# Between attention and experts: counts summed by matmul, steps in another order, slot numbers converted one scatter sooner

## The chip, the cores and the metric

One Trainium2 chip, one core. The metric is device time in microseconds (us) of one execution, the median over runs. The engines are named as in the profile: PE (TensorE), DVE (VectorE), ACT (ScalarE), POOL (GpSimd), SP (the queue that issues most transfers).

## The reference

Three stages follow each other; the output of one is the input of the next.

```
attn = hash_bucket_attention(q, k, v, proj)       # 2 x 8 heads, 768 positions, head size 64
x    = attn as 1536 tokens x 512

logits = x @ w_gate                               # 1536 x 8
e_idx  = argmax(logits)                           # one expert for each token
out[t] = gate_w[t] * sigmoid(x[t] @ w_output_gate)[e_idx] * (relu(x[t] @ w1[e]) @ w2[e])

h = out @ w_in;  solu = h * softmax(h);  y = layernorm(solu) * g_ln @ w_out
```

## The kernel before

The 1536 tokens are 12 tiles of 128. Attention works through 96 units (a head and a block of 128 queries each); three tiles of tokens become ready together, tiles 6 to 8 and then 9 to 11 last. Everything is issued in an order written out by hand, and each engine runs its instructions in that order. The change lies wholly in the stretch between the last attention unit and the first expert, some 10 us long.

In that stretch each token needs its expert and its row ("slot") among the tokens of this expert. The steps, by name:

- `route_a(i)` on DVE: the maximum of the logits and a one-hot row for each token (`oh_all`). The argument is a part: part 2 is tiles 6 to 8, part 3 is tiles 9 and 10, part 4 is tile 11.
- `route_mm(i)` on PE: small matmuls that add up, for each expert, the tokens that come before this one: a triangular matrix times the one-hots, `ones` times `hs` (the counts of earlier parts) and `ones` times single one-hot tiles (the list `before`, L787).
- `route_b(i)` on DVE: picks the own expert's sum from PSUM, which is the slot number (`slot_f`, L803). Then, on POOL and tile by tile, it converts the number to an integer (L809) and starts an indirect scatter (L811) of 128 token rows to `xs` in DRAM.
- `route_s(g)` on DVE: adds the counts of a group of three tiles to `hs` (L822, L823).

Expert 0 does not go through DRAM for tiles 6 to 11. Its input is gathered on PE: `gather_first` (4 matmuls with an identity, L945) brings in what earlier tiles gave, then `gm(t)` (8 matmuls a tile, L952) multiplies the tokens of tile t by a one-hot matrix that `oh(t)` has made (on DVE, L936, or on ACT, two operations at L933 and L934). `gather_copy` copies the four PSUM results out, blocks 0 and 3 on ACT (L963), blocks 1 and 2 on DVE (L961), into `xw`, which `mm1(0, ...)` reads as its moving operand, block 0 first. Expert 1 and later experts read `xs` back through a transposing DMA, `x_load` (L1126); that of expert 1 waits until all scatters have landed.

The PSUM tiles: the gather's blocks 0 and 3 are two banks of one tile of pool `ps_s` (two buffers of two banks, used in turn), blocks 1 and 2 are `ps_t`. The last attention result, `pv`, and `route_mm(4)` have a `ps_s` tile each. When the experts begin, the pool `ps_x` of eight banks takes the place of all of these, and its first tile lies on the first bank of `ps_s`; a tile of the new pool waits for all readers of the old tile that lies below it. The count of `ps_s` allocations (one in `first`, 96 for the units, then `pv`, gather, `route_mm(4)`) puts the gather's tile of this kernel on the first buffer.

After the gather the order is: the four `mm1` groups of expert 0, those of expert 1, `mm2` of expert 0, `mm1` of expert 2, and so on, then the last stage. `fin_*` are the steps that turn a finished attention result into tokens and logits: `fin_hi`/`fin_lo` split it into two halves, `fin_r` takes reciprocals, `fin_mm` multiplies by the gate weights, `fin_l` and `fin_x` scale logits and tokens.

Of the kernel before, what the change touches and what calls it, by code (L numbers as in the profile page):

```python
# [8 lines left out]
F32 = mybir.dt.float32  # L9
F16 = mybir.dt.float16  # L10
I32 = mybir.dt.int32
# [10 lines left out]
def kernel(  # L22
# [15 lines left out]
    nc = tc.nc  # L38
# [3 lines left out]
    E, _, FF = w1.shape  # L42
    NS = S // 128
    NTILE = NT // 128
# [6 lines left out]
    CAP = 224  # L51
# [15 lines left out]
    const = ctx.enter_context(tc.tile_pool(name="const", bufs=1))  # L67
# [5 lines left out]
    xs = dram.tile([E * NT, 2 * DM], F16, name="xs")  # L73
# [5 lines left out]
    ones16 = const.tile([128, 128], F16, name="ones16")  # L79
# [5 lines left out]
    hs = const.tile([128, 5, E], F16, name="hs")  # L85
    oh_all = const.tile([128, NTILE, E], F16, name="oh_all")
    slot_f = const.tile([128, NTILE], F32, name="slot_f")
    slot_all = const.tile([128, NTILE], I32, name="slot_all")
    me = const.tile([128, NTILE, 2], F32, name="me")
    pos_all = const.tile([128, NTILE], I32, name="pos_all")  # L90
    tok = const.tile([128, NTILE], I32, name="tok")
# [210 lines left out]
    scattered = []  # L302
# [9 lines left out]
    def attention(es):  # L312
# [326 lines left out]
        def emit_pv(x):  # L639

            n, blk, qt, _ = units[pairs[x][0]]
            j = 2 * n + blk
            last = x == NU // 2 - 1
            if last:
                pv[j, 2] = ps_s.tile([128, 2, 512], F32, tag="s", name="s")[:, 0]
            elif qt == 0:
                pv[j, 0] = ps_v.tile([128, SB], F32, tag="v", name="v")
            o = pv[j, 2][:, 0:128] if last else pv[j, 0][:, qt * 128:(qt + 1) * 128]
            vt = ldt[n, "v"]
            ph = [pt.pop(i) for i in pairs[x]]  # L650
            for c in range(NS):
                for h in range(2):
                    nc.tensor.matmul(o[64 * h:64 * h + 64], vt[:, h, c], ph[h][:, c],  # L653
                                     start=(c == 0), stop=(c == NS - 1), tile_position=(0, 64 * h))
# [117 lines left out]

        rmm = {}

        def route_mm(i, before=(), tail=False, own=False):

            t0, nt = parts[i]
            if own:
                m = ps_s.tile([128, 2, 512], F32, tag="s", name="s")[:, 0]
            elif tail:  # L780
                m = ps_v.tile([128, 512], F32, tag="v", name="v")
            else:
                m = ps_m.tile([128, 512], F32, tag="m", name="m")
            oh = oh_all[:, t0:t0 + nt]
            nc.tensor.matmul(m[:, 0:nt * E], upper, oh, start=True, stop=False)
            for t in before:
                nc.tensor.matmul(m[:, 0:nt * E], ones16, oh_all[:, t:t + 1].to_broadcast([128, nt, E]),  # L787
                                 start=False, stop=False)
            nc.tensor.matmul(m[:, 0:nt * E], ones16, hs[:, min(i, 3), None].to_broadcast([128, nt, E]),
                             start=False, stop=(nt == 1))  # L790
            for t in range(1, nt):
                nc.tensor.matmul(m[:, t * E:nt * E], ones16,
                                 oh[:, t - 1:t].to_broadcast([128, nt - t, E]), start=False, stop=(t == nt - 1))
            rmm[i] = m

        def route_b(i, before=()):
            t0, nt = parts[i]
            d = nc.vector
            m = rmm.pop(i)
            oh = oh_all[:, t0:t0 + nt]  # L800
            pr = t3("rpr", nt, E, bufs=1)
            for t in range(nt):
                d.scalar_tensor_tensor(out=pr[:, t], in0=m[:, t * E:(t + 1) * E], scalar=1.0, in1=oh[:, t],  # L803
                                       op0=ALU.mult, op1=ALU.mult, accum_out=slot_f[:, t0 + t:t0 + t + 1])
            for f in before:
                f()
            for t in range(nt):
                so = slot_all[:, t0 + t:t0 + t + 1]
                nc.gpsimd.tensor_scalar(out=so, in0=slot_f[:, t0 + t:t0 + t + 1], scalar1=1.0, scalar2=1.0,  # L809
                                        op0=ALU.mult, op1=ALU.mult)  # L810
                x = nc.gpsimd.indirect_dma_start(  # L811
                    out=xs[:, :], out_offset=bass.IndirectOffsetOnAxis(ap=so, axis=0),
                    in_=xh[divmod(t0 // 3, 2)][:, t0 % 3 + t].rearrange("p a b -> p (a b)"), in_offset=None).ins
                for y in scattered:
                    tc.declare_no_dep(x, y, reason="every token has a row of its own")
                scattered.append(x)

        def route_s(g):
            d = nc.vector
# [213 lines left out]
    with tc.manual_schedule():  # L1033
        with ExitStack() as es:
            A = attention(es)
            pj = A["pj"]
            cm, rb, rg = A["cm"], A["rb"], A["rg"]
            setup_first()
            A["first"]()
            A["load"](1)  # L1040
            A["at"](2, setup_late)
            NU = A["NU"]
            bg = A["bg"]
            JL = 2 * NP - 2
            a_ = A.__getitem__
            pv, fa, tr = a_("emit_pv"), a_("fin_a"), a_("emit_t")
            due = a_("due")
            J = JL + 1
            for i in range(NU):
                a_("emit_s")(i, a_("steps_t")(i - 2) if 2 <= i else iter(()))  # L1050
                due(i, 0)
                a_("emit_max")(i)
                due(i, 1)
                if i == NU - 1:
                    tr(NU - 2)
                a_("emit_exp")(i)
                if i == 5 or i >= 6 and i % 2 == 0:
                    pv(i // 2 - 2)
                due(i, 2)
            assert not bg, bg.keys()  # L1060

            oh, gm = a_("gather_oh"), a_("gather_mm")
            pv(NU // 2 - 2)
            a_("fin_l")(JL)
            a_("fin_x")(JL)
            a_("fin_r")(J, 0, 2)
            a_("fin_hi")(J, 0, 2, True)
            tr(NU - 1)
            a_("fin_lo")(J, 0, 2)
            a_("fin_mm")(J, 0, 2)  # L1070
            a_("route_a")(2)
            pv(NU // 2 - 1)
            a_("fin_hi")(J, 2, 3, True)
            a_("gather_ps")()
            a_("gather_first")(range(4))
            a_("route_mm")(2, tail=True)
            a_("fin_l")(J, 0, 2)
            a_("fin_x")(J, 0, 2, True)
            a_("fin_r")(J, 2, 3)
            a_("fin_lo")(J, 2, 3)  # L1080
            a_("route_b")(2)
            a_("fin_mm")(J, 2, 3)
            oh(6)
            oh(7, True)
            a_("route_s")(2)
            gm(6, range(4))
            a_("route_a")(3)
            oh(8, True)
            a_("route_mm")(3, tail=True)
            a_("fin_l")(J, 2, 3)  # L1090
            gm(7, range(4))
            a_("route_a")(4)
            gm(8, range(4))
            a_("route_mm")(4, (9, 10), tail=True, own=True)
            a_("route_b")(3)
            oh(9)
            oh(10, True)
            lo = a_("fin_x")(J, 2, 3, True, True)
            gm(9, range(4))
            a_("route_b")(4, before=(lambda: oh(11), lo))  # L1100
            gm(10, range(4))
            a_("route_s")(3)
            gm(11, (0, 3, 1, 2))
            a_("totals_mm")()
            a_("route_d")(0, 0, 1)
            a_("gather_copy")()
            a_("totals")()
            for x in range(2):
                a_("route_d")(x + 1, 0, 1)
            for x in range(3):  # L1110
                a_("route_d")(x, 2, 3, 4)
# [41 lines left out]
        def overflow():  # L1153
            why = "made on the chip from token counts"
            n = nc.values_load(win[:, 3:4], min_val=0, max_val=MW, skip_runtime_bounds_check_because=why)
            with tc.If(n != 0), tc.For_i(0, n, 1) as i:
# [48 lines left out]
                for a in range(2):  # L1205
                    nc.vector.tensor_copy(out=yT[:, a, :, bass.ds(c0, WIN)], in_=yt[:, a * KD:(a + 1) * KD])

        def mm1(e, g, n):
            w = wt["w1", e].rearrange("p a (k f) -> p a k f", k=KD)
            xw = xw_t[e][..., 0:n]  # L1210
            if g == 0:
                hh_t[e] = mp.tile([128, 2, KF, CAP], F16, tag="hh", name="hh")
            ps = ps_a.tile([128, 2, CAP], F32, tag="a", name="a")
            for i in range(2):
                fs = slice((2 * g + i) * 128, (2 * g + i + 1) * 128)
                for kk in range(KD):
                    nc.tensor.matmul(ps[:, i, 0:n], w[:, 0, kk, fs], xw[:, 0, kk], start=(kk == 0), stop=False)  # L1217
                    nc.tensor.matmul(ps[:, i, 0:n], w[:, 0, kk, fs], xw[:, 1, kk], start=False, stop=False)  # L1218
                    nc.tensor.matmul(ps[:, i, 0:n], w[:, 1, kk, fs], xw[:, 0, kk], start=False, stop=(kk == KD - 1))  # L1219
            return ps  # L1220
# [287 lines left out]
```

## Time and profile before

| | |
|---|---|
| median of 3 runs | 514.83 us (514.05 to 515.08) |
| the profiled execution, its own time | 513.23 us |
| its span, first to last instruction | 511.5 us |
| granted PE clock, mean | 0.999 |
| PE busy | 496.9 us, 97% of the span |
| DVE, ACT, POOL busy | 388.2, 320.9, 281.9 us |

PE is the engine that runs nearly all the time. Busy time of PE overlaps from one matmul to the next, so what counts in the rows below is the start of each matmul and the idle time in square brackets, with the instruction that ended it.

### The profile page before, as it was taken

Reading aid. Unit: us, or ns where it says so; the run is one execution under the profiler, and the core shown is the slowest. Engines: PE = TensorE matmul, PEld = TensorE weight load, DVE = VectorE, ACT = ScalarE, POOL = GpSimd, SP = SyncE. Lnnn points to the kernel's source line nnn. Section 1 sums busy time; section 2 is a strip of 40 time slices with the busy share of each in tenths; the row PEclk is TensorE's granted clock in tenths of the full one; section 3 lists DMA queues with packets and bytes.
Section 4 is the critical chain, followed back from the end, with each engine's and each line's share of the span. In section 5 each row is a group of like instructions: output and inputs, shape, how many; then the busy total and the mean of one; then the engine's idle time right before and its main releaser. Section 6 shows DMA issues by size and latency. Waiting matters only on the chain. (4 is left out here: it accounts for less than half of the span.)

```text
span 511.5 us, 12503 instructions
## 1 busy us (share of the span) xinstructions
PE 496.9 (97%) x4716; PEld 385.1 (75%) x4716; DVE 388.2 (76%) x922; ACT 320.9 (63%) x601; POOL 281.9 (55%) x438
## 2 busy tenths in 40 slices
PE   7899999999999999999999999999999999999994
PEld 5678787888888887887999999999984444444443
DVE  7787888888889888877779799979935987656610
ACT  6778787887887788886256566556623445534421
POOL 6999897869879898644366587322012113221131
PEclk9999999999999999999999999999999999999999
DMA  7398969772946675500499999998800246442281
GB/s 263 57 214 185 245 162 232 195 204 78 187 142 108 187 202 121 161 1 22 157 305 278 318 309 271 268 324 277 279 12 0 42 82 97 108 106 62 62 145 41
DMA packets 107182, 83.21 MB, mean 163 GB/s; under 512 B 80624, under 2 KB 89456, under 8 KB 107120
## 3 DMA queue, kind: packets, MB, share of 16 engines
q1 hardware_dynamic: 104816, 76.09, 59.1%
q0 software_dynamic: 2304, 6.31, 3.2%
q8 instruction: 37, 0.61, 0.5%
q14 instruction: 25, 0.20, 0.1%
HBM read 51.43 MB, written 9.97 MB: 120 GB/s over the span
## 5 line engine op out<-in xcount | busy, mean ns | idle before, releaser
L629 PE MATMUL t<-ident,p 128*128 128x128 f32 x576 | 126.1, 275 | 0.6
L617 ACT ACTIVATE p<-s,mx 128x768 f32<-128x768 f32 x96 | 95.8, 998 | 36.4 <-DVE mx L606 22.5
L602 DVE TENSOR_REDUCE mx<-s 128x1 f32<-128x768 f32 x96 | 91.5, 953 | 28.4 <-PE s L592 22.4
L631 ACT COPY pt<-t 128x384 f32<-128x384 f32 x192 | 85.6, 480 | 7.4 <-PE t L629 6.2
L629 PEld LDWEIGHTS t<-ident,p 128*128 128x128 f32 x576 | 77.8, 141 | 15.6 <-ACT pt L631 9.0
L653 PE MATMUL v<-pt,v 128*64 128x128 f32 x1128 | 72.0, 277 | 0.0
L653 PEld LDWEIGHTS v<-pt,v 128*64 128x64 f32 x1128 | 60.6, 137 | 7.7 <-issue 6.8
L1446 PE MATMUL o<-wo,zT 128*128 128x512 f16 (+1 forms) x312 | 63.7, 363 | 0.1
L1246 PE MATMUL a<-hh,wb 128*128 128x224 f16 (+5 forms) x256 | 63.4, 251 | 0.1
L131 POOL TENSOR_SCALAR dm<-dm 128x512 f32<-128x512 f32 x16 | 33.0, 2061 | 55.5 <-ACT dm L126 55.3
L1374 PE MATMUL h<-wi,yT 128*128 128x512 f16 x288 | 63.5, 379 | 0.0
L1247 PE MATMUL a<-hh,wb 128*128 128x224 f16 (+5 forms) x256 | 63.4, 251 | 0.0
L1248 PE MATMUL a<-hh,wb 128*128 128x224 f16 (+5 forms) x256 | 63.4, 251 | 0.0
L592 PE MATMUL s<-k,q 128*128 128x384 f16 x192 | 59.0, 329 | 1.2 <-ACT p L617 1.2
L592 PE MATMUL s<-b,cm 128*128 128x384 f16 x192 | 57.2, 326 | 0.9 <-DVE b L554 0.9
L1219 PE MATMUL a<-xw,wa 128*128 128x224 f16 (+5 forms) x224 | 55.1, 249 | 0.0
L1218 PE MATMUL a<-xw,wa 128*128 128x224 f16 (+5 forms) x224 | 55.1, 249 | 0.0
L1217 PE MATMUL a<-xw,wa 128*128 128x224 f16 (+5 forms) x224 | 55.1, 249 | 0.0
L1446 PEld LDWEIGHTS <-zT 128*128 128x128 f16 x312 | 30.5, 98 | 32.2 <-issue 0.4
L1374 PEld LDWEIGHTS <-yT 128*128 128x128 f16 x288 | 28.2, 98 | 33.7
L1452 POOL DMA_INDIRECT out_dram<-o,tok x12 | 12.6, 1048 | 53.3 <-issue 42.4
L168 ACT ACTIVATE wb<-raw 128x1024 f16<-128x1024 f32 x24 | 25.3, 1055 | 22.1 <-DMA raw<-in_moe_w_dram 22.0
(275 smaller groups left out, 1017.7 us busy)
## 6 DMA issues: line engine op xcount, KB each, us to landing
raw<-in_moe_w_dram SPq DMA_DIRECT2D x64, 512.0 KB, 6.1
raww<-in_moe_w_in_dram SPq DMA_DIRECT2D x8, 512.0 KB, 5.1
raww<-in_moe_w_out_dram SPq DMA_DIRECT2D x8, 512.0 KB, 6.4
xs<-raw SPq DMA_DIRECT2D x8, 448.0 KB, 4.4
v<-in_v_dram SPq DMA_DIRECT2D x8, 384.0 KB, 6.7
q<-in_q_dram SPq DMA_DIRECT2D x6, 384.0 KB, 4.3
k<-in_k_dram SPq DMA_DIRECT2D x6, 384.0 KB, 6.5
cm<-q SPq DMA_DIRECT2D x14, 96.0 KB, 2.1
```

Source lines behind the costliest of these rows:

```text
L592: nc.tensor.matmul(t[:, c, 0:SB], d[x, h][:, s], flat(d[y, h])[:, c * SB:(c + 1) * SB], start=first, stop=not first)
L602: nc.vector.tensor_reduce(out=mx[:, 0:1], in_=t[:, :, 0:SB], op=ALU.max, axis=AX.XY)
L617: nc.scalar.activation(out=p, in_=s_t.pop(i)[:, :, 0:SB], func=AF.Exp, scale=mx[:, 1:2], bias=mx[:, 2:3], accum_out=sums[j][:, qt, h:h + 1])
L629: nc.tensor.transpose(t[:, g * 128:(g + 1) * 128], p[:, c, g * 128:(g + 1) * 128], ident)
L631: nc.scalar.copy(out=pt[i][:, 3 * c:3 * c + 3], in_=t[:, 0:SB].rearrange("p (g c) -> p g c", g=3))
L653: nc.tensor.matmul(o[64 * h:64 * h + 64], vt[:, h, c], ph[h][:, c], start=(c == 0), stop=(c == NS - 1), tile_position=(0, 64 * h))
L1217: nc.tensor.matmul(ps[:, i, 0:n], w[:, 0, kk, fs], xw[:, 0, kk], start=(kk == 0), stop=False)
L1246: nc.tensor.matmul(ps, w[:, 0, f, ds], hh[:, 0, f], start=(f == 0), stop=False)
L1247: nc.tensor.matmul(ps, w[:, 0, f, ds], hh[:, 1, f], start=False, stop=False)
L1248: nc.tensor.matmul(ps, w[:, 1, f, ds], hh[:, 0, f], start=False, stop=(f == KF - 1))
L1374: nc.tensor.matmul(ps[:, c], yT[:, a, kk, ts], w_i[:, w, kk, c * 512:(c + 1) * 512], start=(kk == 0 and a == 0 and w == 0), stop=(kk == KD ...
L1446: nc.tensor.matmul(ps, zT[:, KF * a + f], w_o[:, w, f, cs], start=(f == 0 and a == 0 and w == 0), stop=(f == KF - 1 and a == 1))
```

## The change

In the stretch named above:

1. `route_mm(2)` is issued ahead of `gather_first`, not behind it. On DVE `route_b(2)` and `oh(6)` come ahead of `fin_r` and `fin_lo` of tile 11; `gm(6)` comes ahead of `fin_mm` of tile 11 on PE.
2. `route_s(2)` moves from between `oh(6)` and `route_a(3)` to the end, just ahead of `route_s(3)`. So `hs` lacks the counts of tiles 6 to 8 when `route_mm(3)` and `route_mm(4)` run, and they add them by matmuls: three more each.
3. The gather's PSUM tile is taken ahead of the last `pv` tile, so the two swap buffers; `route_mm(4)` uses the second bank of the `pv` tile instead of a tile of its own. The first three PSUM tiles of expert 0 are taken together and used in the order second, third, first.
4. For tiles 6 to 11 POOL converts the slot numbers of the next tile before it starts the scatter of a tile. Ahead of the last scatter it writes one element with a `memset`.

```
-                pv[j, 2] = ps_s.tile([128, 2, 512], F32, tag="s", name="s")[:, 0]
+                m = ps_s.tile([128, 2, 512], F32, tag="s", name="s")
+                pv[j, 2], pv[j, 2, 1] = m[:, 0], m[:, 1]
...
-        def route_mm(i, before=(), tail=False, own=False):
+        def route_mm(i, before=(), tail=False, own=None):
-            if own:
-                m = ps_s.tile([128, 2, 512], F32, tag="s", name="s")[:, 0]
+            if own is not None:
+                m = pv[own, 2, 1]
...
-            nc.tensor.matmul(m[:, 0:nt * E], ones16, hs[:, min(i, 3), None].to_broadcast([128, nt, E]),
+            nc.tensor.matmul(m[:, 0:nt * E], ones16, hs[:, min(i, 2), None].to_broadcast([128, nt, E]),
...
-            for t in range(nt):
-                so = slot_all[:, t0 + t:t0 + t + 1]
-                nc.gpsimd.tensor_scalar(out=so, in0=slot_f[:, t0 + t:t0 + t + 1], scalar1=1.0, scalar2=1.0,
+            for t in range(t0, t0 + nt):
+                nc.gpsimd.tensor_scalar(out=slot_all[:, t:t + 1], in0=slot_f[:, t:t + 1], scalar1=1.0, scalar2=1.0,
                                         op0=ALU.mult, op1=ALU.mult)
...
+                if i < 2:
+                    scatter(t)
+                else:
+                    if held:
+                        scatter(held.pop())
+                    held.append(t)
+            if t == NTILE - 1:
+                nc.gpsimd.memset(slot_all[0:1, NTILE:NTILE + 1], 0)
+                scatter(held.pop())
+
+        held = []
+
+        def scatter(t):
+            x = nc.gpsimd.indirect_dma_start(
+                out=xs[:, :], out_offset=bass.IndirectOffsetOnAxis(ap=slot_all[:, t:t + 1], axis=0),
+                in_=xh[divmod(t // 3, 2)][:, t % 3].rearrange("p a b -> p (a b)"), in_offset=None).ins
...
             a_("route_a")(2)
+            a_("gather_ps")()
             pv(NU // 2 - 1)
             a_("fin_hi")(J, 2, 3, True)
-            a_("gather_ps")()
+            a_("route_mm")(2, tail=True)
             a_("gather_first")(range(4))
-            a_("route_mm")(2, tail=True)
             a_("fin_l")(J, 0, 2)
             a_("fin_x")(J, 0, 2, True)
+            a_("route_b")(2)
+            oh(6)
+            oh(7, True)
+            gm(6, range(4))
             a_("fin_r")(J, 2, 3)
             a_("fin_lo")(J, 2, 3)
-            a_("route_b")(2)
             a_("fin_mm")(J, 2, 3)
-            oh(6)
-            oh(7, True)
-            a_("route_s")(2)
-            gm(6, range(4))
+            oh(8, True)
+            gm(7, range(4))
             a_("route_a")(3)
-            oh(8, True)
-            a_("route_mm")(3, tail=True)
+            a_("route_mm")(3, (6, 7, 8), tail=True)
             a_("fin_l")(J, 2, 3)
-            gm(7, range(4))
+            gm(8, range(4))
             a_("route_a")(4)
-            gm(8, range(4))
-            a_("route_mm")(4, (9, 10), tail=True, own=True)
+            a_("route_mm")(4, range(6, 11), tail=True, own=J)
             a_("route_b")(3)
             oh(9)
             oh(10, True)
...
             gm(10, range(4))
+            gm(11, (0, 3, 1, 2))
+            a_("route_s")(2)
             a_("route_s")(3)
-            gm(11, (0, 3, 1, 2))
             a_("totals_mm")()
...
+        ps0 = [ps_a.tile([128, 2, CAP], F32, tag="a", name="a") for _ in range(3)]
+        ps0 = ps0[1], ps0[2], ps0[0]
...
-            ps = ps_a.tile([128, 2, CAP], F32, tag="a", name="a")
+            ps = ps0[g] if e == 0 and g < 3 else ps_a.tile([128, 2, CAP], F32, tag="a", name="a")
```

## Rows read from the trace of the kernel before

**Rows 1.** Stretches: us, busy PE, PEld, DVE, ACT, POOL, PE clock, DMA share, GB/s.

```profile
250.00:255.00 5.00, 5.00 (x55) 5.00 (x53) 3.15 (x34) 1.19 (x8) 0.00 (x0) 1.00 0.48 102
330.00:367.00 37.00, 37.00 (x463) 36.93 (x461) 33.29 (x44) 24.69 (x36) 8.79 (x6) 1.00 0.92 287
367.00:500.00 133.00, 132.72 (x730) 67.22 (x728) 81.51 (x202) 54.42 (x81) 26.25 (x37) 1.00 0.37 79
```

**Rows 2.** Waits of PE from 236 to 256 us: total, times, longest.

```profile
PE a L1217 <- ACT raw L963: 0.7, 1, 0.7
PE s L952 <- DVE raw L936: 0.5, 1, 0.5
PE v L785 <- DVE oh_all L770: 0.3, 1, 0.3
```

**Rows 3.** Timeline of PE: start us, us, line, out<-in, count, [idle before <-releaser].

```profile
237.91 0.36 PE L945 MATMUL s<-raw,ident 128*128 128x448 f16 x1
...
238.67 0.18 PE L785 MATMUL v<-oh_all,upper 128*128 128x24 f16 x1
...
242.46 0.19 PE L787 MATMUL s<-oh_all,ones 128*128 128x8 f16 x2
...
242.62 0.35 PE L952 MATMUL s<-raw,xh 128*128 128x224 f16 x2
...
244.92 0.17 PE L859 MATMUL m<-hs,ones 128*128 128x8 f16 x1
245.75 0.26 PE L1217 MATMUL a<-raw,wa 128*128 128x224 f16 x1 [0.67 <-ACT raw L963]
...
264.15 0.26 PE L1246 MATMUL a<-hh,wb 128*128 128x224 f16 x1
```

**Rows 4.** Timeline of DVE, same columns.

```profile
238.03 0.16 DVE L689 TENSOR_SCALAR r<-sums 128x2 f32<-128x2 f32 x1
...
238.36 0.29 DVE L679 SCALAR_TENSOR_TENSOR xt<-s,xt 128x128 f16<-128x128 f32 x1
238.97 0.17 DVE L803 SCALAR_TENSOR_TENSOR rpr<-v,oh_all 128x8 f32<-128x8 f32 x1 [0.32 <-PE v L792]
...
239.23 0.35 DVE L936 TENSOR_SCALAR raw<-raw,slot_f 128x224 f16<-128x224 f16 x1
239.50 0.17 DVE L822 TENSOR_REDUCE hn<-oh_all 128x8 f16<-128x24 f16 x1
...
239.78 0.16 DVE L762 TENSOR_REDUCE rmx<-lt 128x2 f32<-128x16 f32 x1
...
242.07 0.49 DVE L936 TENSOR_SCALAR raw<-raw,slot_f 128x224 f16<-128x224 f16 x1
...
244.93 1.16 DVE L961 CAST raw<-t 128x448 f16<-128x448 f32 x2 [0.51 <-PE t L952]
...
262.58 0.61 DVE L1226 SCALAR_TENSOR_TENSOR hh<-a,hh 128x448 f16<-128x448 f32 x1
```

**Rows 5.** Timeline of ACT, same columns.

```profile
240.75 0.48 ACT L934 ACTIVATE raw<-y,one 128x224 f16<-128x224 f32 x1
...
244.73 0.97 ACT L963 CAST raw<-s 128x448 f16<-128x448 f32 x2 [0.23 <-PE s L952]
```

**Rows 6.** Timeline of POOL, same columns: first conversion, first and last scatter.

```profile
239.47 0.19 POOL L809 TENSOR_SCALAR slot_all<-slot_f 128x1 int32<-128x1 f32 x1
239.95 1.08 POOL L811 DMA_INDIRECT xs<-xh,slot_all  x1 [0.28 <-POOL slot_all L809]
...
247.73 1.00 POOL L811 DMA_INDIRECT xs<-xh,slot_all  x1 [0.28 <-POOL slot_all L809]
```

**Rows 7.** Last scatter and expert 1's load: issue us; median us to landing.

```profile
xs<-xh,slot_all POOLq DMA_INDIRECT x1, 2.8
...
250.75 1.70 SPq L1126 DMA_TRANSPOSE xw<-xs  x1
...
xw<-xs SPq DMA_TRANSPOSE x1, 4.1
```

More of the change, by code (lines that the diff above doesn't have):

```diff
@@ L87 @@
     slot_f = const.tile([128, NTILE], F32, name="slot_f")
-    slot_all = const.tile([128, NTILE], I32, name="slot_all")
+    slot_all = const.tile([128, NTILE + 1], I32, name="slot_all")
     me = const.tile([128, NTILE, 2], F32, name="me")
@@ L806, in route_b @@
                 f()
-            for t in range(nt):
-                so = slot_all[:, t0 + t:t0 + t + 1]
-                nc.gpsimd.tensor_scalar(out=so, in0=slot_f[:, t0 + t:t0 + t + 1], scalar1=1.0, scalar2=1.0,
+            for t in range(t0, t0 + nt):
+                nc.gpsimd.tensor_scalar(out=slot_all[:, t:t + 1], in0=slot_f[:, t:t + 1], scalar1=1.0, scalar2=1.0,
                                         op0=ALU.mult, op1=ALU.mult)
[L811 to L816, printed above, removed]
+                if i < 2:
[12 more added lines that the diff above has]
+                in_=xh[divmod(t // 3, 2)][:, t % 3].rearrange("p a b -> p (a b)"), in_offset=None).ins
+            for y in scattered:
+                tc.declare_no_dep(x, y, reason="every token has a row of its own")
+            scattered.append(x)
         def route_s(g):
```

## The prediction

> **What bounds the kernel now.** I read the stretches first, because PE's 97% is only an average. From 250 us to the last stage PE has no gap: 5.00 of 5.00, 37.00 of 37.00, 132.72 of 133.00 us [rows 1]. No transfer, DVE or ACT holds the expert stage up, so what moves the start of expert 0 moves the end by the same amount, as long as everything that PE reads is there when it comes earlier. The waits of PE then show where time is to be had at all: between 236 and 256 us it waited three times, 0.7, 0.5 and 0.3 us, 1.5 us in all [rows 2]. The whole change can thus win no more than about 1.5 us, less what can't be hidden.
>
> Two chains lie in the stretch. One goes through DVE: it makes the slots and one-hot matrices that the gather on PE waits for. The other goes through POOL: six scatters one after the other, 239.47 to 248.73 us (the last starts at 247.73 and takes 1.00) [rows 6]. The last lands 2.8 us after its start, at 250.53; SP starts expert 1's load at 250.75 and it lands 4.1 us later, at 254.85 [rows 7]. PE issues 192 matmuls of experts 0 and 1 from 245.75 to 264.15, one per 0.0958 us, so it begins expert 1 at 254.95 [rows 3]. The load is there 0.10 us before PE wants it: whatever makes PE earlier by more than that is lost unless the scatters are earlier too.
>
> **The DVE chain.** `route_mm(2)` starts at 238.67 and `gather_first` at 237.91 [rows 3]; swapped, `route_mm(2)` is 0.76 us earlier, its one-hots being ready. DVE waited 0.32 us for it and began `route_b(2)` at 238.97 [rows 4]; the result would now be there at 238.21. DVE is free at 238.03, where `fin_r` began. From there to `route_a(3)` at 239.78 it spent, start to start, 0.33 on `fin_r`, 0.29 on `fin_lo` (to 238.65), 0.32 waiting, 0.26 on `route_b(2)`, 0.27 on `oh(6)` and 0.28 on `route_s(2)`: 1.75 us [rows 4]. After the change: 0.18 waiting, 0.26, 0.27, 0.33, 0.29: 1.33 us, so `route_a(3)` begins at 239.36. That is 0.42 us won: 0.28 from the moved `route_s(2)`, 0.14 from the wait.
>
> Does the 0.42 reach PE? The rest of DVE's order, up to `oh(9)`, is the same. `oh(9)` ends at 242.07 + 0.49 = 242.56 and `gm(9)` starts at 242.62 [rows 3, 4]: PE runs there right behind DVE. ACT's `oh(7)` and `oh(8)` follow `route_b(2)` and come earlier with it; `oh(8)` ended at 241.23 [rows 5] and would end near 240.5, when PE is still at `gm(7)`. So `gm(9)` starts at 242.20, the 24 matmuls of tiles 9 to 11 end their issue at 244.50 instead of 244.92 [rows 3], and the copies start 0.42 us earlier.
>
> The six added matmuls are of the kind of L787: two issue in 0.05 us (242.46 to 242.51, with the next), so six cost 0.15 us. They run while PE waits for `oh(9)`, in a gap of some 0.3 us; without that cover they cost 0.15. Lower bound 0, upper 0.15; I take 0, because DVE is what `gm(9)` waits for. `route_s(2)` at the end puts 0.28 us on DVE ahead of `gather_copy`, where DVE sat idle 0.51 us [rows 4]; 0.23 is left. ACT's idle time there is 0.23 us [rows 5], and the exponentials ahead of its copies follow DVE's steps; with 0.28 us more in front it is late by 0.05 at worst.
>
> **The copies.** The first matmul of expert 0 waited 0.67 us, and its releaser is ACT's copy, which ran 244.73 to 245.70 for two blocks [rows 3, 5]. The matmul reads block 0 alone, copied by about 245.22; it started at 245.75, behind the second. The reason is the PSUM bank: expert 0's first tile lies on the gather's own tile and waits for both its readers. After the change the gather has the second `ps_s` buffer and the first tile used is the second bank of the `pv` tile, whose readers are long done. So the wait is for one copy: start 245.22 + 0.05 - 0.42, about 244.85. But DVE's second copy (block 2) ends at 244.93 + 1.16 = 246.09 [rows 4], 245.67 after the shift; PE wants block 2 after six matmuls, at 245.43, and waits to 245.72. Before it read block 2 at 245.75 + 0.57 = 246.32. Net gain at this point: 0.60 us, of which 0.42 is the chain and 0.18 the bank. If the bank buys nothing, 0.42.
>
> **The scatters.** A tile takes (247.73 - 239.95)/5 = 1.56 us: conversion 0.2, scatter 1.0, small gaps, and 0.28 us in which the scatter waits for its own conversion [rows 6]. With the next conversion in between, the wait is over when the scatter comes up. The first scatter stays at 239.95 (0.28 behind its conversion, in which the second now fits); the other five follow at 1.28 us, and the `memset`, priced like a conversion, stands where the seventh conversion would. Last start 239.95 + 5 x 1.28 = 246.35, end 247.35 against 248.73. The load of expert 1 then lands near 253.5, and PE, at 254.95 - 0.60 = 254.35, has 0.8 us in hand. No trace shows a scatter that does not stand right behind its own conversion, so the price is open: upper bound of the period 1.56 (the gap belongs to every scatter) with one conversion more in front, lower 1.28. I take 1.28 because the gap's releaser is the conversion.
>
> [...]
>
> **Downstream.** PE comes 0.60 us earlier to everything, DVE's and ACT's steps 0.42. The nearest meeting is the `mm2` of expert 0, at 264.15: its first PSUM tile is the bank that expert 0's third group used (the first group's, before), last read by DVE from 262.58 to 263.19 [rows 3, 4]. PE would come at 263.55, DVE be done at 262.77: 0.78 us in hand, 0.36 if DVE gained nothing. I cost it at 0.
>
> **Sum.** 513.23 - 0.60 = 512.6 us for an execution like the profiled one, whose span is 511.5. That execution is 1.6 us under the median of 514.83, so on the scale of the median: 514.2 us, 0.12% less. Here 0.2% is 1.03 us, about what a measurement of this kernel can tell from no change.
>
> **Rivals.**
>
> - *PE's waits go altogether* (faster). If `oh(9)` takes 0.35 us like `oh(6)` and not 0.49 [rows 4], and the block order hides the copies, all of the 1.5 us goes but about 0.15 (ACT's first copy ends that much behind PE's last matmul of the stretch, 245.22 against 244.92 + 0.17) and 0.15 for the added matmuls: 1.2 us, 513.6. For it: 0.49 is the longest of its kind. Against it: DVE's steps are a chain, and the change shortens it by 0.42 only. Chance 0.14.
> - *The gap stays* (the change does not do what it says). If 0.28 us belongs to every scatter, the chain ends one conversion, 0.24 us, later than before, expert 1's load lands at 255.1, and PE loses its 0.60 us and 0.15 more waiting there: 515.0. It decides as soon as the scatters end later than 248.2. For it: all scatters show the gap. Against it: the releaser named. Chance 0.10.
> - *Scatters get longer* (slower). The first, at 239.95, took 1.08 us, the last 1.00 [rows 6]. If back to back each took the gap's 0.28 more on top of a gap that stays, the chain would end 0.24 + 6 x 0.28 = 1.9 us later and the load would land at 256.8: PE stands 1.8 us at expert 1, 516.6. It crosses 0.2% when the chain ends over 1.1 us late. Nothing in the rows asks for it. Chance 0.04.
> - *DVE and POOL in each other's way.* `oh(9)`, beside a scatter, took 0.49 us, `oh(6)` 0.35 [rows 4]. Should `oh(6)`, now earlier, take the longer time, DVE's chain loses 0.14: gain 0.46, 514.4. [...] Chance 0.10.
>
> **Chances and range.** The forecast, a gain of 0.3 to 0.9 us, has 0.62. Its own range is 513.9 to 514.5. The rivals on both sides reach from 513.6 to 515.0 without the long scatters; medians of three runs of this kernel scatter by some 0.4 us (514.05 to 515.08 for single runs), so the range is 513.3 to 515.2. Faster by over 0.2%: the first rival's 0.14 and 0.08 of the forecast, whose upper end with that scatter lies near 1.03: 0.22. Slower by over 0.2%: 0.04 and 0.02 of the gap that stays: 0.06. Within 0.2%: 0.72.
>
> **What would show it.** Right: `route_b(2)` on DVE near 238.2, `route_a(3)` near 239.4, `gm(9)` near 242.2 with PE waiting for DVE's `oh(9)`, the first matmul of expert 0 near 244.9 and a new wait of some 0.3 us inside its first group; scatters 1.28 us apart, the last ending near 247.4; expert 1 beginning near 254.35 without a wait. Wrong: a wait of PE at expert 1 for the load (the scatters), a first matmul still behind both ACT copies (the bank), `gm(7)` or `gm(8)` waiting for ACT (the chain went over to ACT), or a new gap at `mm2` of expert 0.

## The result, and the profile after

The changed kernel took 519.79 us (median of 6 runs, 518.11 to 520.98), the kernel before 514.37 (6 runs, 513.79 to 515.08): a ratio of 1.0102, 95% interval 1.0081 to 1.0123. (Ratios here and below are those on record for the whole set of runs; they need not be the quotient of the two medians.) It is slower by 1%. The forecast was 514.2.

The stretches of the profiled execution (518.11 us, span 516.3) show where; columns as in [rows 1], where 250 to 255 has PE at 5.00 and the clock at 1.00.

```profile
240.00:245.00 5.00, 4.36 (x53) 3.92 (x50) 3.45 (x25) 1.96 (x6) 4.40 (x7) 1.00 0.39 153
245.00:250.00 5.00, 1.67 (x10) 1.37 (x11) 1.75 (x6) 0.97 (x2) 2.50 (x5) 0.64 0.42 161
250.00:255.00 5.00, 5.00 (x37) 4.31 (x36) 4.64 (x37) 0.48 (x4) 0.00 (x0) 0.67 0.67 144
```

PE stands still for most of 245 to 250, and the clock granted to it falls to 0.64 and 0.67 of full speed on the mean: in the trace it is 1.00 up to 246.44, 0.50 from there to 253.27, and 1.00 again. Lines from the timeline of the same stretch, all engines, are next.

```profile
238.18 0.17 DVE L804 SCALAR_TENSOR_TENSOR rpr<-v,oh_all 128x8 f32<-128x8 f32 x1
...
239.10 0.16 DVE L763 TENSOR_REDUCE rmx<-lt 128x2 f32<-128x16 f32 x1
...
241.41 0.27 PE L788 MATMUL s<-oh_all,ones 128*128 128x8 f16 x5
...
241.46 0.28 DVE L949 TENSOR_SCALAR raw<-raw,slot_f 128x224 f16<-128x224 f16 x1
...
241.54 0.17 PE L790 MATMUL s<-hs,ones 128*128 128x8 f16 x1
...
241.79 0.35 PE L965 MATMUL s<-raw,xh 128*128 128x224 f16 x2
...
242.80 0.17 DVE L804 SCALAR_TENSOR_TENSOR rpr<-s,oh_all 128x8 f32<-128x8 f32 x1 [0.87 <-PE s L790]
...
243.74 0.55 PE L965 MATMUL t<-raw,xh 128*128 128x224 f16 x4
...
244.26 0.18 PE L872 MATMUL m<-hs,ones 128*128 128x8 f16 x1
...
247.32 0.97 ACT L976 CAST raw<-s 128x448 f16<-128x448 f32 x2 [2.62 <-remote]
...
247.36 0.62 DVE L974 CAST raw<-t 128x448 f16<-128x448 f32 x1 [2.73 <-remote]
248.33 0.35 PE L1233 MATMUL a<-raw,wa 128*128 128x224 f16 x1 [3.89 <-remote]
...
248.77 0.62 DVE L974 CAST raw<-t 128x448 f16<-128x448 f32 x1 [0.79 <-remote]
```

Up to 241.8 all is as forecast or earlier: `route_b(2)` at 238.18, `route_a(3)` at 239.10, `gm(9)` (L965) at 241.79. PE starts the 24 matmuls of `gm(9)` to `gm(11)` and then `totals_mm` (L872) at full pace, the last at 244.26, 0.66 us sooner than [rows 3]. Then comes the odd part. `route_mm(4)`'s last matmul (L790) starts at 241.54, but DVE, which waits for it, goes on at 242.80. ACT and DVE, which wait for the gather, start their copies at 247.32 and 247.36, 3.3 us after its last matmul started (244.02, the last of the four at 243.74); in the kernel before ACT started at 244.73 [rows 5], while the last were still going out. The matmuls start in time; that they are done is counted late. I call this late completions. "remote" is the profile's word for a release that it can't trace back to an instruction.

How a late completion is seen needs a remark: the end of a matmul in such rows is modelled, so only who waits for it shows it. Here L790's row ends at 241.71 and its waiter goes on 1.09 us later. The trace also holds the times at which the semaphore that PE counts up changed: for L790 242.78, for the gather's last groups 247.29, 247.34 and 248.75, for `totals_mm` 248.78, that is 1.24 and then 3.5 to 4.7 us after their starts. In the kernel before it is 0.18 for L789, the same matmul there, and 0.27 for the gather. Whether the matmuls themselves finished late or only their count came late, no row tells for certain; it speaks for the count that the first `mm1` matmul had started, at 248.33, before the one of the gather behind which it stands was counted, at 248.75.

The sum: the first matmul of `mm1` starts at 248.33 instead of 245.75 (2.58 us). `mm1(1)`, expert 1's, begins 96 matmuls later, at 259.92 instead of 254.95: 11.59 us for the 96 instead of 9.20, 2.39 us for the lower clock: at 0.50 the matmuls of `mm1` start 0.19 us apart, at 1.00 again 0.096. Together 4.97 us; the two profiled executions differ by 4.88. I take the clock for the consequence: it fell in a stretch in which PE had had next to nothing to do since 244.44, the end of `totals_mm`'s row (244.26 + 0.18), and in the runs below it goes with the wait. Where the first `mm1` waits 2.9 us or more (runs 1, 3, 4, 13, 15 and 16), the mean clock of 250 to 255 is 0.57 to 0.89; in all other profiles, with 1.92 us at most, it is 1.00.

The scatters came closer, as meant:

```profile
239.93 1.08 POOL L824 DMA_INDIRECT xs<-xh,slot_all  x1
...
242.82 1.01 POOL L824 DMA_INDIRECT xs<-xh,slot_all  x1 [0.16 <-issue]
...
246.94 0.97 POOL L824 DMA_INDIRECT xs<-xh,slot_all  x1 [0.21 <-POOL slot_all L818]
...
249.94 1.47 SPq L1139 DMA_TRANSPOSE xw<-xs  x1
```

(246.94 - 239.93)/5 is 1.40 us a scatter instead of 1.56 [rows 6], and each takes what it took before. The last line is expert 1's load.

### The profile page after: what moved, and what is told of

Same layout as the page of the kernel before. It is cut to its first block, busy times and chain, and to the rows that moved or that the text cites. A ratio compares the mean times of both kernels' runs of the same rounds, so it can differ in the third digit from the quotient of the medians.

```text
span 516.3 us, 12515 instructions
## 1 busy us (share of the span) xinstructions
PE 500.4 (97%) x4722; PEld 387.3 (75%) x4722; DVE 388.5 (75%) x922; ACT 321.6 (62%) x601; POOL 281.3 (54%) x439
```

## The experiments

There were 18 runs, in six groups, some of them of one kernel; the kernels of a group ran on one chip beside runs of the kernel before. Groups 1 and 2 had the same chip. Theory A: the added matmuls on the ones matrix hold PE back. Theory B: the scatters, closer together, hold its completions back. Theory C: the new order or the PSUM tiles do.

**Group 1: the parts alone.** Run 1, the kernel before with part 4 of the change alone, as its diff stands above:

> The kernel before with the scatters' part of the change alone (slot numbers converted one scatter sooner). Theory A (the loss of 5 us comes from TensorE: the six added matmuls on the ones matrix and the clock of 0.64 that follows) expects no loss here: 514.0 to 514.6, the last scatters 1.41 instead of 1.56 us apart, no wait of mm1 above 1 us. Theory B (the scatters, once closer together, hold back TensorE's or the DMA's completions) expects the loss here: 518 to 520, with the clock near 0.64 in 245-250.

Run 2, the change without that diff:

> The changed kernel with the old scatters (convert, then scatter). Theory A: the loss stays, 518 to 520.5, with the granted clock near 0.64 in 245-250. Theory B: the loss goes, 514 to 515.

Run 3, the change without the added matmuls:

```
-            a_("route_mm")(3, (6, 7, 8), tail=True)
+            a_("route_mm")(3, tail=True)          # hs[min(i, 3)], route_s(2) after oh(7)
-            a_("route_mm")(4, range(6, 11), tail=True, own=J)
+            a_("route_mm")(4, (9, 10), tail=True, own=J)
```

> The changed kernel with the six added matmuls taken out: the counts of tiles 6 to 8 are summed on VectorE again ahead of the logits of tile 9, all else as changed. Theory A: the loss goes, 513.8 to 514.8, clock 1.00 in 245-255. Theory C (the new order, or route_mm(4) in the second bank of pv's tile, holds TensorE's completions back): the loss stays, 518 to 520.

Run 4, the change with the tiles of part 3 as before (`gather_ps` behind `pv` again, too):

```
-        ps0 = ps0[1], ps0[2], ps0[0]
...
-                m = pv[own, 2, 1]
+                m = ps_s.tile([128, 2, 512], F32, tag="s", name="s")[:, 0]
```

> The changed kernel with the old PSUM tiles (a tile of its own for route_mm(4), the gather's tile allocated after pv's, the first mm1 in turn), all else as changed. Theory A: 518 to 520.5, as changed. Theory C in its form with the bank: 514 to 515.

Measured, the kernel before at 516.51 us: run 1 519.84 (ratio 1.0071, 1.0046 to 1.0096), run 2 516.44 (1.0007, 0.9980 to 1.0033), run 3 517.93 (1.0043, 1.0014 to 1.0072), run 4 521.02 (1.0103, 1.0053 to 1.0153). Theory A falls with run 1: without one added matmul its first `mm1` waits longest. It falls with run 3 too, which has none of them either and still waits 2.9 us.

```profile
249.15 0.97 ACT L975 CAST raw<-s 128x448 f16<-128x448 f32 x2 [3.76 <-remote]
...
250.17 0.35 PE L1229 MATMUL a<-raw,wa 128*128 128x224 f16 x1 [4.74 <-ACT raw L975]
```

Those rows are run 1's timeline. Theory C in its form with the tiles falls with run 4, which is as slow with the old tiles. In its form with the new order it is not needed for the loss, since run 1 has the old order. Run 2 speaks for B, but its first `mm1` still waits 1.92 us, though its scatters are nearly as far apart as in the kernel before (1.54 us); so the new order may add to it:

```profile
246.95 0.26 PE L1221 MATMUL a<-raw,wa 128*128 128x224 f16 x1 [1.92 <-ACT raw L964]
```

And the kernel before now scattered from 513.39 to 519.53: something else had changed.

**Group 2: what of the scatters.** Run 5, run 6, run 7 (the kernel before), run 8:

```
+            if t < 6:
...
+            else:
+                x = nc.gpsimd.dma_start(out=xs[128 * t:128 * (t + 1), :], in_=src).ins   # run 5
...
+                for _ in range(3 if t >= 6 else 1):     # run 6: the conversion of tile t
...
+                for _ in range(2 if t0 >= 6 else 1):    # run 7: the same
...
+                in_=xh[(0, 1) if t >= 6 else divmod(t // 3, 2)][:, t % 3].rearrange("p a b -> p (a b)"), in_offset=None).ins  # run 8
```

> The changed kernel with the last six scatters replaced by plain transfers of the same rows to fixed rows, issued from the same place on GpSimd; the rows of xs are then not where the reference wants them. Theory B1 (GpSimd's making of the scatters' descriptors, once every 1.41 us, holds TensorE's completions back): the wait of the first mm1 falls from 3.9 us to under 1, clock 1.00 in 245-255, 512 to 515. Theory B2 (the transfers themselves, 256 KB each, hold them back): the loss stays, 518 or more.

> The changed kernel with each of the last six slot conversions done three times, which puts the scatters some 1.9 us apart instead of 1.41. Theory B (the spacing decides): TensorE's completions are on time, the wait of the first mm1 under 1.5 us, 513.5 to 516, the clock 1.00. Theory A (the count matmuls and the order): 518 to 520.5 as changed.

> The kernel before with each of the last six conversions done twice, the scatters some 1.85 us apart instead of 1.56. Theory B: the kernel before, which lay between 513.4 and 519.5 on the last chip, stays near its fast end, 513.5 to 515.5. If the spread has another source, it stays as wide and the median near 516.

> The changed kernel with the last six scatters reading an older tile of x that TensorE doesn't read at that time, so wrong rows go out, as many and as often. Theory B3 (the scatters read the tile that the gather matmuls read as weights, and the two collide): the loss goes, 514 to 515. Theories B1 and B2: it stays, 518 to 520.5.

Measured, the kernel before at 516.35: 515.80 (0.9973, 0.9942 to 1.0005), 517.96 (1.0023, 1.0002 to 1.0044), 518.53 (1.0029, 1.0001 to 1.0057), 515.47 (0.9996, 0.9970 to 1.0022). No profile of this group has a late completion, runs 6 and 7 with scatters 1.83 and 1.88 us apart no more than run 8 with 1.42; so the group says nothing on the spacing. Runs 6 and 7 pay otherwise: their last scatters start at 249.99 and 249.66, expert 1's load comes late, and PE waits 2.6 and 2.7 us for it. Run 8 seemed to say that the scatters must not read what PE reads. Its profiled execution is what the forecast had in mind: 512.76 us, `mm1(1)` at 254.25.

**Group 3: the yardsticks again.** Run 9, the changed kernel, and run 10, the kernel before, both as they are; run 11 as run 8; run 12 with `x2 = xh[0, 1][:, sub]` as the gather's weights:

> The changed kernel unchanged, so that the next ones have their yardstick in the same company. Every theory: 518 to 521, TensorE's last gather group counted 3 us after its matmuls were issued, the first mm1 3.9 us late. Should it come out near 514 instead, the loss isn't a property of the program alone, and what was read from single profiles so far has to be taken back.

> The kernel before unchanged. If its slower executions (up to 519.5) have the same stall as the changed kernel, a profile of one of them shows TensorE's completions late by 1 to 4 us between 241 and 249; if their time goes elsewhere, the completions are on time (0.2 us after the last start) and mm1's first wait is 0.7 us.

> The changed kernel with the last six scatters reading an older tile of x (wrong rows go out), once more. Theory B3 (scatters and gather matmuls collide on one tile): 512.7 to 515, no late completion, at least 4 us below the changed kernel. If it lies within 1 us of the changed kernel, the source of the scatters has no part in it.

> The changed kernel with the gather matmuls taking their weights from an older tile of x instead of the one that the scatters read (expert 0's gathered rows are then wrong). Theory B3: the loss goes, 512.7 to 515. Theory B1 (GpSimd's descriptors): it stays, 518 to 521.

Measured, the kernel before at 517.09: 515.88 (0.9987, 0.9961 to 1.0012), 516.69 (1.0005, 0.9970 to 1.0040), 515.90 (0.9990, 0.9965 to 1.0015), 515.12 (0.9980, 0.9959 to 1.0001). The changed kernel is not slower here. No profile of this group has a late completion either. So the reading of run 8 falls: the changed kernel is as fast without its edit, runs 11 and 12 had no loss to remove, and no run tests the source of the scatters where completions are late. The loss is not the program's alone. Run 9's timeline, the same program as in the result:

```profile
241.62 0.28 DVE L949 TENSOR_SCALAR raw<-raw,slot_f 128x224 f16<-128x224 f16 x1
...
241.71 0.17 PE L790 MATMUL s<-hs,ones 128*128 128x8 f16 x1
...
241.95 0.35 PE L965 MATMUL s<-raw,xh 128*128 128x224 f16 x2
...
242.01 0.16 DVE L804 SCALAR_TENSOR_TENSOR rpr<-s,oh_all 128x8 f32<-128x8 f32 x1
...
244.04 0.34 ACT L854 ACTIVATE rex<-rdf 128x24 f32<-128x24 f32 x2 [1.15 <-DVE rdf L850]
...
244.28 0.17 PE L872 MATMUL m<-hs,ones 128*128 128x8 f16 x1
...
244.29 0.97 ACT L976 CAST raw<-s 128x448 f16<-128x448 f32 x2
...
245.31 0.26 PE L1233 MATMUL a<-raw,wa 128*128 128x224 f16 x1 [0.86 <-ACT raw L976]
```

Up to 242.01 the two executions agree within half a microsecond; there one counts on time and the other doesn't. Run 10, a slow execution of the kernel before (521.07 us), shows where its time goes. Its waits from 300 to 375 us (total, times, longest) and a stretch of it:

```profile
ACT wb L168 <- DMA raw<-in_moe_w_dram: 21.5, 14, 3.1
...
PE a L1217 <- DVE hh L1226: 3.1, 1, 3.1
...
PE a L1219 <- DVE wa L172: 1.2, 2, 0.9
```

```profile
300.00:325.00 25.00, 25.00 (x278) 25.00 (x276) 19.16 (x25) 13.44 (x18) 16.57 (x16) 1.00 0.99 252
```

In the execution shown ahead of the prediction PE has no wait there, and the same two lines read:

```profile
ACT wb L168 <- DMA raw<-in_moe_w_dram: 15.7, 11, 3.4
```

```profile
300.00:325.00 25.00, 25.00 (x278) 25.00 (x277) 22.90 (x30) 13.75 (x20) 17.51 (x16) 1.00 1.00 295
```

Run 9 has 1.6 us of PE waits there. Run 10's `mm1(1)` begins at 255.05, on time; then PE waits 4.3 us, and the granted clock is 0.86 in 350 to 375 (1.00 in run 9). In run 10 the expert weights come more slowly, and that, not the stretch of the change, makes it late.

One thing that all executions with late completions share is in the trace too. A transfer of this kernel leaves 16 landing records: the 289 of the execution shown ahead of the prediction left 4,621, 3 short of 289 x 16. In the result's profile and in group 1, 170 to 200 of some 4,620 are missing; in groups 2 and 3 at most 14 are. Against run 9, the result's lacks 59 at 140 to 158 us and 64 at 240 to 252, where scatters run, and nearly all others after 252. I don't know what the condition is; it came and went with the group, and not with the chip, which groups 1 and 2 share.

**Group 4: side by side.** Run 13, the changed kernel, and run 14, the kernel before, unchanged:

> The changed kernel unchanged, once more. If the loss belongs to the program under a condition that comes and goes, it is either 518 to 521 with TensorE's last gather group counted 3 us late, or 514 to 517 with it counted on time, and nothing in between.

> The kernel before, beside the run above. Where the changed kernel's completions are late: if the kernel before's are late too (by 1 us or more), the condition hits both and only the amount differs; if they are on time, its wider spacing of the scatters keeps it clear. Where the changed kernel's are on time, these are too, and its time differs from the changed kernel's only by how long TensorE waits for expert weights between 300 and 370.

Measured, the kernel before at 516.76: 518.69 (1.0021, 0.9990 to 1.0051) and 517.14 (1.0006, 0.9977 to 1.0035). Records are missing in both. The changed kernel's first `mm1` waits 3.9 us, that of the kernel before 0.7. Run 13 and, below it, run 14:

```profile
247.47 0.97 ACT L976 CAST raw<-s 128x448 f16<-128x448 f32 x2 [2.95 <-remote]
...
248.48 0.34 PE L1233 MATMUL a<-raw,wa 128*128 128x224 f16 x1 [3.89 <-ACT raw L976]
```

```profile
244.53 0.97 ACT L963 CAST raw<-s 128x448 f16<-128x448 f32 x2 [0.24 <-PE s L952]
...
245.55 0.26 PE L1217 MATMUL a<-raw,wa 128*128 128x224 f16 x1 [0.67 <-PE m L859]
```

So under one condition the late completions hit the changed kernel and spare the kernel before, as far as one profile of each shows it. That the ratio is smaller than in the result, and its interval holds 1, goes in part with the weights: run 14 waits 1.4 us in 300 to 375, run 13, 5.75 us later at `mm1(1)`, not at all, and the two profiled executions differ by 3.15 us.

**Group 5: the spacing, a miss.** Runs 15 (the change) and 16 (run 1), each with a fill ahead of every late scatter:

```
         def scatter(t):
+            if t >= 6:
+                nc.gpsimd.memset(slot_all[0:1, NTILE:NTILE + 1], 0)
```

> The changed kernel with a one-element fill on GpSimd ahead of each of the last six scatters, which puts them some 1.55 us apart instead of 1.41. Theory B4 (the spacing decides, under the condition in which landing records are missing): the first mm1 waits about 1 us instead of 3.9, the last gather group is counted on time, 514 to 517. If the spacing has no part: 516.8 to 519.6 as in the last run, mm1's wait 3.9. Where no landing records are missing, both give 514 to 517 and the run tells nothing on this.

> The kernel before with the scatters' part alone and the same fill ahead of each scatter. Theory B4: as the kernel before, mm1's wait 0.7 us, 514 to 518. If it is the order of conversion and scatter and not the spacing: mm1's wait 4.7 us and 519 to 520 again. Where no landing records are missing, it tells nothing on this.

Measured, the kernel before at 517.78: 517.99 (1.0007, 0.9984 to 1.0030) and 519.06 (1.0040, 1.0021 to 1.0059); records are missing. The fill ran in the gap that was there anyway, and the spacing became 1.44 and 1.43 us, not 1.55; the waits fell to 3.2 and 3.3. Nothing is decided by that alone.

**Group 6: the spacing, beyond the old one, and the transfers.** Run 17, and run 18 as run 5:

```
+                for _ in range(2 if 8 <= t <= 10 else 1):     # run 17: the conversion of tile t
```

> The changed kernel with the slot conversions of tiles 8 to 10 done twice: the first three gaps between scatters are some 1.7 us instead of 1.4, the last two stay short, and the last scatter starts where it does in the kernel before. Theory B4 (spacing): with landing records missing, mm1's first wait is about 1 us instead of 3.9, TensorE's last gather group is counted within 0.5 us of its last start, mm1(1) begins by 255, and the time is that of the kernel before or 0.5 us under it. If the spacing has no part: mm1's wait 3 us or more, 517 to 520.

> The changed kernel with plain transfers to fixed rows in place of the last six scatters (the rows of xs are then not where the reference wants them), which run at 0.6 to 1.1 us apart. If the transfers and their landings hold TensorE's completions back, mm1's first wait is 4 us or more, since they come closer together than in any other run; if it is GpSimd's making of descriptors for indirect scatters, the wait is 1 us, whether landing records are missing or not.

Measured, the kernel before at 516.72: run 17 515.87 (0.9974, 0.9951 to 0.9997), run 18 515.32 (0.9976, 0.9950 to 1.0001). Run 17's timeline:

```profile
239.78 1.08 POOL L825 DMA_INDIRECT xs<-xh,slot_all  x1
...
241.52 1.01 POOL L825 DMA_INDIRECT xs<-xh,slot_all  x1
...
243.19 1.01 POOL L825 DMA_INDIRECT xs<-xh,slot_all  x1
...
243.97 0.17 PE L873 MATMUL m<-hs,ones 128*128 128x8 f16 x1
...
244.06 0.97 ACT L977 CAST raw<-s 128x448 f16<-128x448 f32 x2
...
244.86 1.01 POOL L825 DMA_INDIRECT xs<-xh,slot_all  x1
245.08 0.26 PE L1234 MATMUL a<-raw,wa 128*128 128x224 f16 x1 [0.94 <-ACT raw L977]
...
254.67 0.26 PE L1234 MATMUL a<-xw,wa 128*128 128x224 f16 x1 [0.23 <-DMA xw<-xs]
```

Records are missing in it as in the others, yet its first `mm1` waits 0.94 us and ACT copies 0.09 us after `totals_mm` (L873) starts; all that its later scatters cost is 0.23 us at expert 1's load. All runs with missing records, worked out from their traces:

```
kernel                          landing   spacing of six     first mm1    mm1(1)
                                records   scatters, mean us  waits, us    begins
changed, as in the result        4434       1.40               3.89       259.92
run 4, old PSUM tiles            4426       1.40               3.9        260.21
run 1, scatters' part alone      4424       1.41               4.74       260.81
run 13, changed                  4426       1.42               3.9        260.49
run 3, no added matmuls          4425       1.42               2.9        258.48
run 16, run 1 with a fill        4397       1.43               3.3        260.46
run 15, changed with a fill      4434       1.44               3.2        258.84
run 2, changed, old scatters     4451       1.54               1.92       256.15
run 14, before                   4407       1.55               0.67       254.74
run 17, spread, then close       4412       1.56 (1.69 the     0.94       254.67
                                            first three)
run 18, plain transfers          4475       0.81               0.86       255.20
for comparison, records there:
run 9, changed                   4620       1.42               0.86       254.51
shown ahead of the prediction    4621       1.56               0.67       254.95
```

So where records are missing the spacing goes with the loss: run 17 is the changed kernel with three conversions more, and its wait is 0.94 us against 3.9 in run 13. That is one profile of each, on two chips. The mean granted clock of all executions points the same way: it is 0.996 or lower in all ten of run 13, and 0.997 or higher in nine of ten of run 17. The spacing isn't all, since runs 2 and 14 have nearly the same and wait 1.92 and 0.67 us. Run 18 has transfers of the same size closer than any and no late completion. But against run 9 none of its records is missing at 240 to 252, where its transfers are plain; of the 145 that it lacks 44 are at 148 to 154 and 34 at 174 to 190, where its scatters are still indirect. So it may have lacked the condition in the stretch that counts. It points to the indirect scatter itself and not to the bytes, and doesn't show it.

Run 17 is also the only version that is faster than the kernel before by an interval that leaves 1 out, if barely: 0.26%, with 515.87 against 516.72 us. Of 18 runs one can come out so by chance. The changed kernel was not in that group; against the kernel before it stood at 1.0102 and 1.0021 where records were missing and at 0.9987 where they weren't.

## Why the prediction was wrong

**The DVE chain** was right and undersized. I had `gm(9)` at 242.20 with DVE's `oh(9)` at 0.49 us. `oh(9)` began 0.61 us sooner than before (241.46) and took 0.28, and `gm(9)` started at 241.79 (241.95 in run 9), as before some 0.05 us behind its end. `totals_mm` came 0.64 to 0.66 us sooner, not 0.42. With that the premise of the rival *PE's waits go altogether* came true, and its gain did not, because of the copies. *DVE and POOL in each other's way* did not come: the earlier `oh(6)` took 0.27 us, and `oh(9)`, again beside a scatter (241.41 to 242.41), 0.28.

**The six added matmuls**, costed at nothing: it stands. In `route_mm(4)` three of them and the two old ones go out in 0.13 us (241.41 to 241.54). PE is through with them before `oh(9)` is done (L790 starts at 241.71 in run 9, `oh(9)` ends at 241.90), and run 3 lost its time without them.

**The copies** failed. The first `mm1` was to wait for one copy of ACT and start at 244.85. In run 9 it starts at 245.31, behind both (244.29 + 0.97 = 245.26). The bank bought nothing. With it out of the way the first `mm1` still waits for both. In the trace of the kernel before the semaphore that ACT counts up rises once for the two copies, at 245.71, when that of block 3 ends (245.70); and in all rows shown here, of both kernels, the first `mm1` starts 0.04 to 0.05 us behind this end. Nor did the copies keep up with the gather. I had ACT late by 0.05 us at worst through the moved `route_s(2)`; in run 9 the gather's blocks 0 and 3 are counted at 244.08 and ACT, busy with the exponentials (L854), copies at 244.29, 0.21 us later.

**The sum in the stretch** came out by luck. Counted from the start of the last attention unit's last matmul, which takes out what executions differ by before it, `mm1` begins 8.05 us later in the kernel before (8.04 to 8.05 in three profiles) and 7.47 in the changed kernel without late completions (runs 8, 9, 11 and 12). That is 0.58 us won, where the prediction had 0.60. But the chain gave 0.77 instead of 0.42, counted the same way at `totals_mm`, and the copies took 0.19 back instead of giving 0.18.

**The scatters** are the step that the result hangs on. Its sizes were off: the period fell to 1.40 and not to 1.28, since of the gap of 0.28 us 0.16 stays. I had let all of it go because its releaser was the conversion; 0.12 went. That was harmless, the load went out at 249.94 instead of 250.75 [rows 7]. What failed is the assumption behind it: I priced the spacing by expert 1's load alone and took PE's completions to be independent of what POOL issues. Where records are missing they are not (run 1, the scatters' part alone, waits 4.74 us; the kernel before, run 14, 0.67), and that cost 3.0 us of waiting (3.89 against 0.86 in run 9) and 2.4 us of clock. The slower rival had scatters that get longer and a wait at expert 1; they didn't get longer, and the wait was at expert 0.

**Downstream at nothing** held up to expert 1 and not to the end. Counted as above, `mm1(1)` begins 0.57 us sooner in runs 8, 9, 11 and 12 too, without a wait. But "PE has no gap" from 250 on [rows 1] was read from one execution. In later groups PE waits for expert weights, 1.4 (run 14), 3.3 (run 17) and 4.3 us (run 10), and there a gain ahead of it is not seen in the time.

**Open.** What the condition is, and by what way an indirect scatter holds back the count of PE's completions. Missing records and late completions come together but are not one thing: runs 14 and 17 miss as many and are on time. Nor is the edge known: run 2, at 1.54 us, still waits 1.06 us longer than run 9, run 14, at 1.55, no longer than the kernel before ever did; the order of the steps may have a part in it. A rival stays untested: every execution here was recorded, one that isn't was not tried, and the loss may belong to the recording and not to the kernel; no run here tells the two apart.

## What to carry to other kernels

Price a closer spacing of indirect scatters not only by when the last one lands: look at who on other engines must be counted done while they run. If a tight handover lies there, try them spread until it is past and closed up afterwards, as in run 17. When a program is slower by far more than any of its steps can be, run the unchanged kernels again side by side before its parts are blamed: here run 8 explained the loss with a cause that run 9 took away. And a stall on PE can cost twice, once for itself and once for the clock: 3.89 us in the result cost 2.39 more, while behind the 1.92 us of run 2 the 96 matmuls took 9.20 us (246.95 to 256.15), as in the kernel before.

## What was not expected of the hardware

- PE's matmuls started at full pace while their completions were counted up to 4.7 us after their starts instead of 0.27, with indirect scatters 1.40 to 1.44 us apart and landing records missing. With 1.55 us (run 14), 1.69 (run 17, while the gather ran) or plain transfers 0.81 us apart the copies started on time, with 1.54 (run 2) about 1 us late; with records there also 1.42 us was on time (run 9).
- One program, run 9 and the result's: 0.86 and 3.89 us for the same wait, on two occasions.
- A one-element fill of 0.09 us ahead of a scatter lengthened the spacing by 0.03 us (run 15 has 1.44 instead of 1.41 between the second and the third): it ran in a gap that the scatter has anyway.
